# A planned kernel for RWKV-6 attention and a MetaFormer block: new durations of transfers, a new count of TensorE's instructions and a new table of shifts in its planner

## Chip, cores and metric

The kernel runs on one core of one Trainium2 chip. The metric is device time in microseconds of one execution; lower is better. The core has five engines that work side by side: TensorE (PE, with its weight loads shown as PEld), VectorE (DVE), ScalarE (ACT), GpSimd (POOL) and SyncE (SP), which here only issues transfers (DMA). Each engine takes its instructions strictly in the order in which they were written; between engines they wait for each other by semaphores.

## The reference

What is computed, cut to what matters:

```python
# r, k, v, w: (B=4, H=8, S=768, D=48), u: (8, 48)
state = np.zeros((B, H, D, D))
for t in range(S):
    cur = np.einsum('bhd,bhe->bhde', u[None] * kt, vt)
    y[:, :, t] = np.einsum('bhd,bhde->bhe', rt, state + cur)
    state = wt[:, :, :, None] * state + np.einsum('bhd,bhe->bhde', kt, vt)
x = y.transpose(0, 2, 1, 3).reshape(4, 768, 384)
mu, var = x.mean(-1), x.var(-1)            # per token
xn = (x - mu) / np.sqrt(var + 1e-6) * g_ln
out = x + np.maximum(xn @ w_ch1, 0) @ w_ch2   # w_ch1: (384, 1536), w_ch2: (1536, 384)
```

## The kernel before, in words

**Rounds.** The tokens are worked through in eight rounds of 384 tokens (four batches, two halves each). A round has two units of four heads. Round 0 is split into a first tile of 128 tokens and the other 256, so that its names carry the first token tile, as in `h_ps_0_1` (hidden group 0, tiles 1 and 2).

**Attention of a round (`front`).** w, k and r are loaded as they lie (`nat`), turned by TensorE (`w_ps`, `k_ps`, `r_ps`) and copied back by ScalarE. Within a chunk of 64 tokens the products of decays are built in six levels. At each level TensorE makes small products of r and k (`quads`, in the profile `a<-r,k` with 63, 62, 60, 56, 48 or 32 rows, 48 products for a whole round), VectorE multiplies k and r by the decays of that level (`grow`: `k<-k,tot`, `r<-r,tot`), and VectorE keeps the level's squares under a mask (`keep`: `A<-mask,a`). A level's quads need the `grow` of the level before. k is then turned once more (`kn_ps`), `states` makes products of k and v (`a<-v,k`) and a scan on VectorE (`s<-s,decay,a`), and `outputs` adds all up (`a<-v,A`, `a<-sx,rx`, `a<-s,r`). The term with u (`own`: `rk`, `own`, `vo`) needs no TensorE. All these small products use four parts of TensorE's array at a time; the planner calls them `tiled`. They share two homes in PSUM (tag `a`).

**The MLP of a round (`norm`, `mlp`).** VectorE normalises x to `xn`; TensorE turns it (`xT_ps`), ScalarE scales it (`xf`). In round 0 the first product is in float32 (`h_ps<-xf,w`), in later rounds it is made of three products in a rounded format (`hd_ps<-xd,d`, `h_ps<-xhl,wl`, `h_ps<-xhl,wh`), for which the difference weights `d` are streamed from DRAM. The second product is float32 up to round 4 (`o<-ffn,h`) and of three parts in the last three rounds (`a<-w2d,hD` and the like, `o_2D`, `o_2P`). The weights themselves come as pairs of words (`raw`) and are put together by three ScalarE and two VectorE operations each (`convert`: `w<-w,held`, later `ffn<-ffn,rest`).

**The planner.** Nothing is issued in the order of the Python loops. Each operation is given to `plan.add` with an engine (or a choice of VectorE and GpSimd, `EITHER`), a duration, what it reads and writes, an urgency `pri`, and for transfers a latency `lat` and a `size`, the time by which it holds up the transfers behind it. `add` also adds the shift from the table `SHIFTS` whose key is the urgency rounded down. `order` then plays the engines through: of the operations that can start within `WAIT[engine]` of the earliest, it takes the most urgent, and issues it. So each duration, latency, size and shift decides only the order in which each engine's instructions are written.

Four things in `order` matter here. A change of mode on TensorE, between tiled and full products, makes an operation less urgent by `STAY`. Tiled operations are planned `MARGIN` behind their operands. `fetches` models TensorE's instruction supply: every `PIECE` = 256 instructions a new piece has to be there, and a piece takes `FETCH`. And where TensorE would stand still for more than 0.4 us in the first 90 us of the plan, `idle` fills the time with products of zeros (`idle<-nought`), counted in units of 128 columns.

Of the kernel before, what the change touches and what calls it, by code (L numbers as in the profile page):

```python
# [35 lines left out]
class InOrder:  # L36


    waits, last = [], None
# [27 lines left out]
class Plan:  # L67
# [11 lines left out]

    HOP, MARGIN, FILLED, PATIENCE, STAY = 0.1, 0.293159, 60.0, 2.0, 2.0
    BEFORE, PIECE, FETCH, CROWD = 66, 256, 4.11468, 300
    WAITS = 1.006
    DRAIN = {True: 0.1, False: 0.12}
    WAIT = {"PE": 0.0617605, "ACT": 0.155358, "DVE": 0.170848, "POOL": 0.403865, "SP": 0.0}

    SHIFTS = {  # L90
        -232: 14, -216: -4.5, -38: -42, -37: 5, -33: 10.5, -31: -22, -28: -9, -20: 13, -14: -23,
        3: -45, 5: -19.5, 10: -35, 12: 4.5, 14: 4, 21: 8, 22: 29.5, 38: 17.5, 51: 68.5, 52: 30,
        53: -5.5, 54: 24, 55: 4, 58: -30, 62: -4, 63: 26, 66: 2.5, 90: -16, 92: 7.5, 101: -19,
        104: 56, 121: -39, 127: 29.5, 129: 59.5, 136: -23, 142: 8.5, 160: -5, 169: 47, 176:
        -27.5, 182: 14, 207: 7.5, 208: 31, 215: -17.5, 246: 0.5, 247: -12.5, 248: 2.5, 249: -35,
        257: -3.5, 262: 31, 284: 12, 289: 8.5, 306: 4.5, 319: -23.5, 403: 15, 405: 32.5, 409:
        121.5, 412: -52, 417: 8, 418: -16, 425: -2.5, 445: 2.5, 447: 72, 449: -25, 450: -9.5,
        451: 14.5, 454: 3.5, 457: 66.5, 459: 88.5, 462: -10, 463: 5, 479: -74, 483: 8.5, 492: 2,
        493: 22, 497: 64.5, 498: 25.5, 501: 22.5, 502: -8.5,
    }  # L100

    def __init__(self, homes, dynamic):
# [37 lines left out]
    def order(self, busy, idle=None, until=0.0):  # L140
# [16 lines left out]
        dma, todo, out, tiled = 0.0, len(ops), [], False  # L157
        count, ahead = self.BEFORE, 0.0
# [19 lines left out]

        def fetches(t, op):

            waits, after = 0.0, ahead
            for at in range(-int(count) % self.PIECE, op.count, self.PIECE):
                now = t + waits + op.costs["PE"] * at / op.count
                waits += max(after - now, 0.0)
                after = max(now, after) + self.FETCH
            return waits, after

        def switching(t, op):
# [4 lines left out]
        while todo:  # L193
            best = None
            for e, waiting in ready.items():
                at = [(t, op) for op in waiting if (t := start_of(op, e)) is not None]
                if not at:
                    continue
                first = min(t for t, _ in at)
                t, op = min(  # L200
                    ((t, op) for t, op in at if t <= first + self.WAIT[e]),
                    key=lambda x: (x[1].pri + (switching(*x) if e == "PE" else 0), x[1].i),
                )
# [3 lines left out]
            t, op, e = best  # L207
            if idle and e == "PE" and t < until and t - free["PE"] > 0.4 and self.homes[idle[0]]:
                n = int((t - free["PE"]) / (idle[1] * (2 if t < 5.0 else 1)))
# [10 lines left out]
            if e == "PE":  # L220
                fetched, ahead = fetches(t, op)
# [55 lines left out]
def kernel(  # L277
# [12 lines left out]
    nc = tc.nc  # L290
# [11 lines left out]
    U = H // NH  # L302
# [29 lines left out]
    plan = Plan(HOMES | {"a": 2, "b": 4}, ("a", "b"))  # L332
# [107 lines left out]
    def urgent(part, stage):  # L440
        rnd, c0, nc = part
        return at(rnd - (nc == 1), stage)
# [31 lines left out]
    def load_first(nm, part, eng, pri):  # L474
        _, c0, nc = part
        b, f = rounds[0]
        name = natural(nm, part, 0)[0]
        queue = SP if eng == "SP" else ACT
        row, margin = row_of(part)

        def go():
            queue.dma_start(
                out=tiles[name][:, margin : margin + H * row].rearrange("p (h x) -> p h x", h=H),
                in_=SRC[nm][b, :, ds(f * RN + c0 * P, nc * P)]
                .rearrange("h (p c) d -> p h (c d)", p=P),
            )

        plan.add(eng, 0.5, go, w=[name], r=[], pri=pri, lat=2.0, size=0.8 + 0.3 * (nc > 1))

    def load(nm, q):  # L490
        b, f, g = units[q]
        name = f"nat_{nm}{q}"

        def go():
            to = tile_("nat", name, None)
            if q // U < ROWS:
                SP.dma_start(
                    out=to[:, 0 : NH * ROW].rearrange("p (h x) -> p h x", h=NH),
                    in_=SRC[nm][b, ts(g, NH), ds(f * RN, RN)]
                    .rearrange("h (p c) d -> p h (c d)", p=P),  # L500
                )
                return
            for c in range(TT):
                SP.dma_start(
                    out=by_tile(to)[:, c, :, 0:D],
                    in_=SRC[nm][b, ts(g, NH), ds(f * RN + c * P, P)].rearrange("h p d -> p h d"),
                )

        cost_, size = (0.5, 0.8) if q // U < ROWS else (1.65, 1.2)
        plan.add(  # L510
            "SP", cost_, go, w=[name], new=[("nat", name)], pri=at(q // U, "wrk".index(nm)), lat=2.0,
            size=size,
        )
# [309 lines left out]
    def load_v(q, part):  # L823
        _, c0, nc = part
        b, f, g = units[q]
        name, swapped = f"v{q}", f"vx{q}"

        def go():
            t = tile_("v", name, [P, NH, TT, D])
            for c in range(c0, c0 + nc):  # L830
                SP.dma_start(
                    out=t[:, :, c],
                    in_=v[b, ts(g, NH), ds(f * RN + c * P, P)].rearrange("h p d -> p h d"),
                )

        def swap():
            t, src = tile_("vx", swapped, [P, NP, TT, D]), tiles[name]
            cols = slice(c0 * D, (c0 + nc) * D)
            for i in range(2):
                SP.dma_start(  # L840
                    out=t[ds(C * (1 - i), C)].rearrange("p r c d -> p r (c d)")[..., cols],
                    in_=src[ds(C * i, C)]
                    .rearrange("p (r j) c d -> p r j (c d)", j=2)[:, :, 1, cols],
                )

        share = nc / TT
        plan.add(
            "SP", 0.1 + 1.6 * share, go, w=[(name, c0)], new=[] if c0 else [("v", name)],
            pri=urgent(part, 16), lat=2.0, size=share,
        )  # L850
        plan.add(
            "SP", 1.25, swap, r=[(name, c0)], w=[(swapped, c0)], new=[] if c0 else [("vx", swapped)],
            pri=urgent(part, 17), lat=2.3, size=0.3 + 0.7 * share,
        )

    def own_term(q, part):
# [300 lines left out]
    def convert(i):  # L1157
        value_, src, key = parts[i]
        raw_ = f"raw{i}"
# [38 lines left out]

        pri = CONVERT + i / 100
        first = -6 if i < FC // 2 else pri  # L1200
        plan.add("SP", 0.4, fetch, w=[raw_], new=[("raw", raw_)], pri=pri - 24, lat=2.0, size=1.05)
        plan.add(
            "ACT", 0.52, upper, r=[raw_], w=[key], new=[("w2", key)] if i >= FC else [], pri=pri,
        )
# [8 lines left out]
    def halve(g):  # L1213
# [44 lines left out]
        for kc in range(KC):  # L1258
            plan.add(
                "ACT", 0.5, lambda kc=kc: up(kc), r=[rest_[kc]], w=[(l_, kc)],  # L1260
                new=[("w1", l_)] if kc == 0 else [], pri=pri,
            )
            plan.add(
                EITHER, (0.56, 1.1), lambda e, kc=kc: diff(e, kc), r=[(h_, kc), (l_, kc)],
                w=[diff_[kc]], new=[("rest", diff_[kc])], pri=pri,
            )
            plan.add(
                "SP", 0.5, lambda kc=kc: store(kc), r=[diff_[kc]], w=[("w1d", g, kc)], pri=pri,
                lat=2.5, size=1.0,
            )  # L1270

    def halve2(f):
# [59 lines left out]
    def thirds(rnd, f):  # L1332
# [34 lines left out]
        for i in range(TT):  # L1367
# [49 lines left out]
            if last:  # L1417
                plan.add("DVE", 0.53, add, r=[keys[1]] + whole, w=[(x_, "sum", i)], pri=EVICT)
                plan.add("DVE", 0.53, rest, r=[keys[0], (x_, "sum", i)], w=[(x_, "out", i)], pri=EVICT)
                plan.add("SP", 0.36, store, r=[(x_, "out", i)], pri=EVICT, lat=2.0, size=1.0)  # L1420

    def first_product(part):
        rnd, c0, nc = part
# [24 lines left out]
    def mlp(rnd):  # L1448
# [3 lines left out]
        for f in range(FC):  # L1452
# [39 lines left out]
            def relu(h_=h_):  # L1492
# [6 lines left out]
            )  # L1499
            plan.add("ACT", 0.45, copy, r=[ps_d], w=[h_], pri=EVICT)  # L1500
            plan.add(
                "PE", 1.12, go, count=12,
                r=[(f"wl{g}", kc) for kc in range(KC)] + [(f"wh{g}", kc) for kc in range(KC)]
                + [key for kc in range(KC) for key in x_keys(rnd, kc)[:2]]
                + [ps_d if rnd < LAST else ps_d + "t"],
# [9 lines left out]
        for i in range(TT):  # L1515
# [32 lines left out]

            whole = x_of(rnd, i)
            plan.add("DVE", 0.53, add, r=[o] + whole, w=[(x_, "out", i)], pri=EVICT)  # L1550
            plan.add("SP", 0.36, store, r=[(x_, "out", i)], pri=EVICT, lat=2.0, size=1.0)

    def front(part):
# [9 lines left out]
        if rnd == c0 == 0:  # L1565
            plan.add(
                "SP", 0.6, lambda: SP.dma_start(
                    out=u_bc,
                    in_=bass.AP(tensor=u.tensor, offset=u.offset, ap=[[0, P], [D, H], [1, D]]),
                ), w=["u_bc"], pri=5, lat=2.0, size=3.3,  # L1570
            )
            plan.add(
                EITHER, (1.3, 1.6), lambda e: BY[e].memset(a_bufs[1], 0.0), w=[("A1", 0, 0)], pri=32
            )
            for lev in range(NLEV - 1):
                plan.add(
                    "POOL", 1.7, lambda lev=lev: build_mask(lev), r=["wide"], w=[("mask", lev)],
                    pri=lev - 40, port=False,
                )
# [114 lines left out]
```

## Time and profile before

| | us |
|---|---|
| median of three timed runs | 530.34 (530.22 to 533.26) |
| profiled execution | 528.18 |
| its span, on which all times of the profile are counted | 526.2 |
| TensorE busy | 514.0 (8984 products) |
| VectorE busy | 398.5 |
| ScalarE busy | 268.4 |
| GpSimd busy | 82.4 |
| mean granted clock of TensorE | 0.996 |

A row of the profile gives the operation as output<-inputs with the buffers' numbers left out, the shape, and durations. All instructions come from one helper line (L50), so rows are told apart by names. A product in float32 is executed as two passes and is counted as two; a transpose or a product in the rounded format is one. Durations of products on TensorE overlap, so that what one costs is read from start to start: 0.109 us for a transpose of 128 columns, 0.22 for a first product of 128 columns (both passes), 0.43 for one of 256, 0.174 for one of 384 columns in the rounded format. "issue" as the cause of idle time means that the engine waited for nothing that the profile shows.

### The profile page before, as it was taken

How to read it: one execution, taken by the hardware profiler on the slowest of the kernel's cores; microseconds unless marked ns; L12 is line 12 of the kernel's file. 1: busy time of each engine (PE TensorE's matmuls, PEld its weight loads, DVE VectorE, ACT ScalarE, POOL GpSimd, SP SyncE). 2: the span in 40 equal slices, each digit the busy share in tenths (PEclk: the TensorE clock that was granted, in tenths of full speed). 3: DMA queues.
4: the chain of work that ended last, by engine and by line, in shares of the span. 5: the costliest groups of instructions: out<-in, count | busy, mean ns of one | idle time of the engine just before them, and what ended most of it. 6: DMA issues, size and time to landing. Idle time of an engine off the chain costs nothing.

```text
span 526.2 us, 20613 instructions
## 1 busy us (share of the span) xinstructions
PE 514.0 (98%) x8984; PEld 434.7 (83%) x8984; DVE 398.5 (76%) x839; ACT 268.4 (51%) x602; POOL 82.4 (16%) x112
## 2 busy tenths in 40 slices
PE   8999799999999999999999999999999999999996
PEld 6788588677899777899767899758966999999996
DVE  5988959989998998989896597715754876655645
ACT  3788768865385342574440873505930533432321
POOL 6304020071332320131200130000300000000000
PEclk9999989999999999999999999999999999999999
DMA  9855977158836614666401324104201422322201
GB/s 218 249 168 126 224 184 194 31 124 203 244 73 123 161 39 97 134 137 132 133 19 35 94 76 112 34 15 128 57 17 45 123 61 66 99 75 75 77 1 45
DMA packets 122361, 55.83 MB, mean 106 GB/s; under 512 B 93984, under 2 KB 119200, under 8 KB 122272
## 3 DMA queue, kind: packets, MB, share of 16 engines
q1 hardware_dynamic: 119152, 53.54, 40.3%
q10 hardware_dynamic: 3120, 0.98, 0.9%
q8 instruction: 70, 1.15, 0.9%
q14 instruction: 19, 0.16, 0.1%
HBM read 45.05 MB, written 7.10 MB: 99 GB/s over the span
## 4 chain that ended last, share of the span: by engine, by line
PE 93%; DVE 3%; POOL 1%; issue 1%; DMA 1%; ACT 0%; DVEq 0%; POOLq 0%
PE a L50 25%; PE o L50 22%; PE h_ps L50 21%; PE hd_ps L50 9%; PE r_ps L50 3%; PE k_ps L50 3%; PE w_ps L50 3%; PE o_2P L50 2%; PE kn_ps L50 2%; PE xT_ps L50 1%; PE idle L50 1%; PE o_2D L50 1%; DMA nat<-in_k_dram 1%; DVE k L50 1%; POOL rk L50 1%
## 5 line engine op out<-in xcount | busy, mean ns | idle before, releaser
L50 PE MATMUL o<-ffn,h 128*128 128x384 f32 x360 | 123.8, 490 | 0.0
L50 PEld LDWEIGHTS o<-ffn,h 128*128 128x128 f32 x360 | 65.7, 190 | 38.2
L50 ACT COPY h<-hd_ps 128x384 f32<-128x384 f32 x84 | 40.2, 479 | 83.3 <-PE hd_ps L50 79.9
L50 PEld LDWEIGHTS a<-r,k 48*63 48x63 f32 (+5 forms) x4608 | 63.4, 126 | 15.6 <-issue 7.5
L50 PE MATMUL a<-r,k 48*63 48x32 f32 (+5 forms) x4608 | 69.5, 212 | 2.7 <-issue 1.7
L50 DVE SCALAR_TENSOR_TENSOR h<-h_ps,h 128x384 f32<-128x384 f32 x84 | 46.4, 555 | 32.8 <-PE h_ps L50 30.7
L50 PE MATMUL h_ps<-xhl,wl 128*128 128x384 f32 x252 | 59.7, 345 | 0.0
L50 PE MATMUL h_ps<-xhl,wh 128*128 128x384 f32 x252 | 57.7, 336 | 0.0
L50 PE MATMUL hd_ps<-xd,d 128*128 128x384 f32 x252 | 56.5, 349 | 0.0
L50 DVE TENSOR_TENSOR k<-k,tot 112x768 f32<-112x768 f32 (+1 forms) x50 | 40.3, 807 | 8.4 <-PE a L50 5.9
L50 PEld LDWEIGHTS h_ps<-xhl,wh 128*128 128x128 f32 x252 | 45.2, 188 | 0.0
L50 PEld LDWEIGHTS hd_ps<-xd,d 128*128 128x128 f32 x252 | 43.7, 188 | 1.8 <-ACT w L50 0.2
L50 PEld LDWEIGHTS h_ps<-xhl,wl 128*128 128x128 f32 x252 | 44.1, 188 | 1.2 <-ACT r L50 0.2
L50 ACT ACTIVATE h<-h 128x384 f32<-128x384 f32 x48 | 25.1, 525 | 36.6 <-DVE h L50 36.4
L50 DVE COPY_PREDICATED A<-mask,a 128x768 f32<-128x768 int8 (+2 forms) x36 | 39.5, 1096 | 2.5 <-PE a L50 2.3
L50 DVE TENSOR_TENSOR r<-r,tot 112x768 f32<-112x768 f32 (+1 forms) x50 | 39.6, 793 | 0.0
L50 ACT ACTIVATE hH<-h 128x384 fp32r<-128x384 f32 x36 | 18.5, 525 | 32.2 <-DVE h L50 24.4
L50 DVE SCALAR_TENSOR_TENSOR hL<-h,hH 128x384 fp32r<-128x384 f32 x36 | 20.0, 554 | 12.0 <-ACT hH L50 11.5
L50 POOL TENSOR_TENSOR rk<-nat,nat 128x576 f32<-128x576 f32 (+1 forms) x13 | 17.8, 1372 | 65.9 <-DVE ffn L50 20.9
L50 DVE TENSOR_TENSOR x<-o,x 128x384 f32<-128x384 f32 x15 | 8.3, 554 | 25.1 <-PE o L50 25.1
L50 PE MATMUL h_ps<-xf,w 128*128 128x128 f32 (+1 forms) x144 | 27.1, 342 | 0.0
L50 ACT COPY A<-a 32x384 f32<-32x384 f32 (+2 forms) x36 | 15.5, 432 | 19.4 <-PE a L50 19.1
(121 smaller groups left out, 1022.9 us busy)
## 6 DMA issues: line engine op xcount, KB each, us to landing
d<-w1d SPq DMA_DIRECT2D x84, 192.0 KB, 3.0
raw<-in_moe_w_ch_dram SPq DMA_DIRECT2D x24, 384.0 KB, 3.8
v<-in_v_dram SPq DMA_DIRECT2D x48, 96.0 KB, 3.1
out_dram<-x SPq DMA_DIRECT2D x24, 192.0 KB, 2.1
nat<-in_w_dram SPq DMA_DIRECT2D x36, 96.0 KB, 3.5
nat<-in_k_dram SPq DMA_DIRECT2D x36, 96.0 KB, 3.2
nat<-in_r_dram SPq DMA_DIRECT2D x36, 96.0 KB, 3.0
w1d<-w1diff SPq DMA_DIRECT2D x12, 192.0 KB, 2.6
```

The source lines that it names most:

```text
L50: ins = self.tc.keep_in_program_order(f(*args, **kw))
```

## The change

The change edits numbers of the planner, and in `fetches` the way in which the start of the next piece of instructions is counted. `STAY` goes from 2.0 to 6.8, `MARGIN` from 0.293 to 0.197, `PATIENCE` from 2.0 to 4.3; `WAIT` changes for each engine. Most transfers get another `size` (loads of w, k and r 1.6 instead of 1.2 in later rounds, raw weights 1.3 instead of 1.05, v 1.6 instead of 1.0 for a whole round, stores 0.65 instead of 1.0), the first loads another latency (3.5 instead of 2.0). The table `SHIFTS` is replaced as a whole, 77 entries by 92. No operation is added or taken away by hand.

```diff
-    HOP, MARGIN, FILLED, PATIENCE, STAY = 0.1, 0.293159, 60.0, 2.0, 2.0
-    BEFORE, PIECE, FETCH, CROWD = 66, 256, 4.11468, 300
+    HOP, MARGIN, FILLED, PATIENCE, STAY = 0.1, 0.196918, 60.0, 4.33011, 6.79752
+    BEFORE, PIECE, FETCH, CROWD = 66, 256, 3.98109, 300
-    WAIT = {"PE": 0.0617605, "ACT": 0.155358, "DVE": 0.170848, "POOL": 0.403865, "SP": 0.0}
+    WAIT = {"PE": 0.0354766, "ACT": 0.217982, "DVE": 0.140393, "POOL": 0.485775, "SP": 0.0207245}
     SHIFTS = {
-        -232: 14, -216: -4.5, -38: -42, -37: 5, -33: 10.5, -31: -22, -28: -9, -20: 13, -14: -23,
+        -537: -0.5, -535: -6.5, -520: -4, -457: -8, -337: 9.5, -296: 10.5, -295: 5.5, -200: -2,
...
-            waits, after = 0.0, ahead
-            for at in range(-int(count) % self.PIECE, op.count, self.PIECE):
-                now = t + waits + op.costs["PE"] * at / op.count
+            waits, after, n = 0.0, ahead, op.count * self.WAITS
+            at = (self.PIECE - count % self.PIECE) % self.PIECE
+            while at < n:
+                now = t + waits + op.costs["PE"] * at / n
                 waits += max(after - now, 0.0)
                 after = max(now, after) + self.FETCH
+                at += self.PIECE
...
-        plan.add(eng, 0.5, go, w=[name], r=[], pri=pri, lat=2.0, size=0.8 + 0.3 * (nc > 1))
+        plan.add(eng, 0.5, go, w=[name], r=[], pri=pri, lat=2.0 if c0 else 3.5, size=1.05 + 0.5 * (nc > 1))
...
-        cost_, size = (0.5, 0.8) if q // U < ROWS else (1.65, 1.2)
+        cost_, size = (0.5, 1.05) if q // U < ROWS else (1.65, 1.6)
...
-            pri=urgent(part, 16), lat=2.0, size=share,
+            pri=urgent(part, 16), lat=2.0, size=1.6 * share,
-            "SP", 1.25, swap, r=[(name, c0)], w=[(swapped, c0)], new=[] if c0 else [("vx", swapped)],
-            pri=urgent(part, 17), lat=2.3, size=0.3 + 0.7 * share,
+            "SP", 1.3, swap, r=[(name, c0)], w=[(swapped, c0)], new=[] if c0 else [("vx", swapped)],
+            pri=urgent(part, 17), lat=2.2, size=0.2 + 0.5 * share,
...
-        plan.add("SP", 0.4, fetch, w=[raw_], new=[("raw", raw_)], pri=pri - 24, lat=2.0, size=1.05)
+        plan.add("SP", 0.4, fetch, w=[raw_], new=[("raw", raw_)], pri=pri - 24, lat=2.0, size=1.3)
...
-                lat=2.5, size=1.0,
+                lat=2.3, size=0.7,
...
-                plan.add("SP", 0.36, store, r=[(x_, "out", i)], pri=EVICT, lat=2.0, size=1.0)
+                plan.add("SP", 0.36, store, r=[(x_, "out", i)], pri=EVICT, lat=2.0, size=0.65)
...
-                "PE", 1.12, go, count=12,
+                "PE", 1.11 if rnd < LAST else 1.05, go, count=12,
...
-                ), w=["u_bc"], pri=5, lat=2.0, size=3.3,
+                ), w=["u_bc"], pri=5, lat=2.0, size=1.5,
```

## The prediction

> **What bounds the kernel now.** I read the page first, for the share of each engine. TensorE is busy 98% of the span, and its clock is granted in full in every slice but the sixth.
>
> ```profile
> PE 514.0 (98%) x8984; PEld 434.7 (83%) x8984; DVE 398.5 (76%) x839; ACT 268.4 (51%) x602; POOL 82.4 (16%) x112
> ...
> PEclk9999989999999999999999999999999999999999
> ```
>
> So the sum of products bounds it, and only three things can move: TensorE's idle time, its clock, and what its order itself costs. The view of TensorE's waits has the named idle time; its longest entries all lie before 68 us:
>
> ```profile
> PE a L50 <- issue: 1.7, 2, 1.2
> PE k_ps L50 <- DMA nat<-in_k_dram: 1.6, 2, 1.3
> PE a L50 <- DVE r L50: 0.8, 1, 0.8
> ```
>
> TensorE's timeline gives them a place (start, duration, instruction; in brackets the idle time before it):
>
> ```profile
> 60.35 1.39 PE L50 MATMUL a<-r,k 48*60 48x32 f32 x82 [0.78 <-DVE r L50]
> 62.97 0.41 PE L50 MATMUL a<-r,k 48*60 48x32 f32 x14 [1.23 <-issue]
> 63.31 1.56 PE L50 MATMUL h_ps<-xf,w 128*128 128x256 f32 x6
> 66.16 0.61 PE L50 MATMUL k_ps<-ident,nat 128*112 128x128 f32 x2 [1.29 <-DMA nat<-in_k_dram]
> ```
>
> One block waits for VectorE, then in its middle for its own instructions ("issue"), and then TensorE, which takes its work in order, stands before the transposes of k until their load lands. The view by stretches of 3.41 us (length, busy time of PE, PEld, DVE, ACT, POOL, granted clock, DMA share, GB/s) shows what follows:
>
> ```profile
> 61.14:64.55 3.41, 2.18 (x61) 1.85 (x53) 3.17 (x9) 2.02 (x4) 0.00 (x0) 1.00 0.83 172
> 64.55:67.96 3.41, 1.76 (x12) 1.09 (x11) 1.82 (x5) 0.85 (x3) 0.00 (x0) 1.00 0.97 223
> 67.96:71.37 3.41, 3.28 (x17) 2.91 (x16) 1.77 (x3) 1.63 (x6) 0.00 (x0) 0.50 0.86 227
> ```
>
> After the poorly filled stretch the clock is 0.50 for 3.41 us. From start to start, TensorE loses here 0.9 us (VectorE), 1.3 (issue), 2.2 (the load of k: pauses of 1.67, 0.68 and 0.29 us where 0.22, 0.11 and 0.11 are usual) and 1.7 (half of 3.41, the clock): **6.1 us between 59 and 72 us**. From 80 us on, the waits view has only two entries, of 0.3 and 0.2 us. Ahead of 59 us VectorE is the bound: from 10.33 us, when the first w is copied, to 58.65 us, the end of the last normalised tile of round 0, its own waits come to 3.7 us in all.
>
> **What the change does.** No edited number is executed; each moves the planner's order. Of the operations, only TensorE's filler products (idle<-nought) grow, from 12 to 18, and six operations go from GpSimd to VectorE on balance. All 351 transfers and all real products stay, so I sum over the order.
>
> *Start.* The first loads get a planned landing 1.5 us later, so six filler products of 384 columns stand ahead of the first transposes, where two stood. The timeline of the start:
>
> ```profile
> 0.99 2.50 PE L50 MATMUL idle<-nought 128*128 128x384 f32 x4 [0.99 <-DVE eps L50]
> 4.34 1.93 PE L50 MATMUL r_ps<-ident,nat_r 128*112 128x128 f32 x8 [0.85 <-POOL wide L50]
> ...
> 10.33 1.96 PE L50 MATMUL w_ps<-ident,nat 128*112 128x128 f32 x16
> ```
>
> Eight transposes take 1.93 us at 4.34 and sixteen take 1.96 at 10.33: the clock is half until about 10 us. Each filler product is two passes, so there are 12, at about 0.65 us cold (from 2.50 us for four shorter ones) and 0.33 warm. If the clock stayed half until 9.9 us as in this row, they would end at 8.9 us, and the 24 transposes, which ended at 9.5, near 11.9: +2.4 us. The Trainium skill (TensorE: Matmul & The Clock Gate, part "The HAM clock gate") holds instead that about 3.4 us of sustained work release the clock, at a phase that a free-running window sets. The fillers have no pause, where the row has one of 0.85 us; so full speed would come between 4.4 and 7.8 us. With 6.1, about 7.7 passes are cold and 4.3 warm: the end is at 7.5 us, the transposes' at 7.5 + 24 x 0.11 = 10.1. I take the rule, as the row is not uninterrupted work: **+0.6 us** (-0.4 to +2.4).
>
> *VectorE to the end of round 0's normalising.* Added up with the durations of the same forms in the trace, its rows up to that tile are 56.2 us before and 57.1 after, +1.0. Against it, the scans (s) waited 1.4 us for TensorE and 0.4 for ScalarE; conversions of w_2 and w_3 now stand between. I put the two at **0** (-1 to +1.5).
>
> *TensorE's work done by then.* While VectorE holds the pace, TensorE's own work is free. Ahead of the transposes of x it now has three more first products (9 products x 0.22 = 2.0), six transposes fewer (-0.65) and a change of mode more (+0.33, below): **-1.7 us** for all that follows.
>
> *The stall at 60 to 67 us.* In the new order two groups of transposes of w and the first wide product (0.65 + 1.3 us) precede the block that waited 0.9 us for VectorE. Behind that block come three narrow first products (2.0) and a wide one (1.3) before the transposes of k, and their load stands at the same place behind as many others in SP's queue. It landed near 67.1 us; TensorE reaches it near 67.6. So the 2.2 us go. What takes their place: the next block (56x32) is planned only 11 us behind, and VectorE's rows up to its operands, with the conversions of ffn_0 to ffn_3 among them, come to 11.3. I leave 0.9 us there and 1.3 for the issue, of whose price no row with another spacing tells me more (0 to 2). The stretch before k is then filled to 80% or more.
> Does the clock stay? The skill's rule (same page, "HAM oscillation") is that idle gaps over about 3.4 us must be avoided. By the rule nothing is gained here, as the longest gap was 1.29 us and the clock should never have fallen. By the rows, a stretch 52% filled (1.76 of 3.41) was enough, and one 64% filled (2.18) was not. I take the rows: the 1.7 us go. Together 6.1 - 2.4 = **-3.7 us** (by the rule -2.0).
>
> *Changes of mode.* STAY is raised, yet TensorE passes 164 times between small concurrent products (a<-r,k, a<-v,k, a<-v,A) and full ones, where it passed 148 times. The chain of waits shows the price:
>
> ```profile
> 138.56 1.25 PE hd_ps L50 x6
> ...
> 161.96 1.45 PE a L50 x96
> ...
> 173.27 1.51 PE a L50 x96
> ...
> 242.50 2.83 PE a L50 x192
> ...
> 357.11 1.05 PE hd_ps L50 x6
> ```
>
> Six products that follow a small block take 1.25 us, others 1.05: 0.20. Two blocks of these kinds alone take 1.45 + 1.51, joined 2.83: 0.13. That is 0.33 per pair. Eight pairs more, one counted above: 7 x 0.33 = **+2.3 us**. It is on the path, since TensorE is full there.
>
> *Margins.* MARGIN falls from 0.293 to 0.197: each small block is planned 0.1 us nearer to its operands. Up to about 250 us VectorE's summed rows run about 2 us or more ahead of TensorE's in both orders, except at the blocks named, so I put **+0.5 us** (0 to 2). Six operations more on VectorE (0.6 to 1 us each) lie in that lead; without it they would cost up to 5 us.
>
> *End.* Behind the last first product six groups of second products cover VectorE's and ScalarE's last conversions where seven did (0.52 each): 3.1 us against a chain of about 3.3. The last store is reached by the same two VectorE rows: 0 (to +0.5).
>
> **Sum:** +0.6 + 0 - 1.7 - 3.7 + 2.3 + 0.5 + 0 = **-2.0 us**. Against the profiled execution (528.18 us, span 526.2) that is 526.2; the median of the timed runs is 530.34, 2.2 above it, so I forecast **528.3**. About 1% (5.3 us) is what a measurement of this kernel can tell from no change.
>
> **Rivals.**
> *A, the whole head closes.* The clock is released early (-1.0 against my +0.6), the issue stall (1.3), the wait at the 56x32 block (0.9) and the margin (0.5) are nothing as well: -5.7, **524.6**. For it: the issue stalls stand in long runs of small products, which are now more often interrupted. Against it: the seven pairs stay.
> *B, slower: the conversions come in front of TensorE.* VectorE waited 2.9 and 2.5 us for ScalarE's parts of ffn here, behind a full TensorE. In the new order ffn_0 to ffn_3 stand ahead of the operands of the 56x32 block, and ScalarE does part of it only after copies that wait for TensorE. If these 5.4 us come onto the path for the 0.9 (+4.5), the stretch is empty again and the clock falls (+1.7), and the start costs 1.2: -2.0 + 6.8 = +4.8, and with the longer fillers +5.4, **535.7**. It decides from a wait of 2.9 us at that block on: there the gain is used up. Against it: ScalarE is busy for only 2.7 of the 8 us from 64 to 72.
> *C, the load of k stays late.* Earlier small loads push it behind again; 2.2 and 1.7 stay: +1.9, **532.2**. For it: the DMA share is 0.83 to 0.97 there. Against it: the same number of transfers stands ahead.
> That the change does nothing is excluded: the orders part from TensorE's eleventh group on.
>
> **How the numbers follow.** Forecast 0.52, A 0.20, B 0.14, C 0.14. Most of A lies below 525.0: with a little of the forecast's tail, faster 0.20. B straddles 535.6, and unseen stalls add to it: slower 0.14. The rest is 0.66. The range takes in most of A and C and the start's bad end, and leaves half of B out: 523.8 to 534.5; the forecast's own is 526 to 531.
>
> **What would show it.** Right: no entry for a load of k among TensorE's waits, granted clock 1.00 from 60 to 80 us, first block of small products near 10.3 us, TensorE some 4 to 5 us further by 80 us, and about 2.3 us of it given back later in groups of 1.25 us. Wrong: a clock of 0.50 after 20 us, a wait of over 2 us for VectorE near 70 us, or idle time of TensorE behind 100 us.

## The result, and the profile after

| | before | after |
|---|---|---|
| median of eight timed runs, us | 530.28 (527.78 to 533.26) | 527.97 (526.07 to 530.06) |
| profiled execution, us | 528.18 | 526.92 |
| its span, us | 526.2 | 525.2 |
| mean granted clock in it | 0.996 | 1.000 |
| TensorE busy, us (products) | 514.0 (8984) | 515.8 (8996) |
| VectorE busy, us | 398.5 | 403.6 |
| GpSimd busy, us | 82.4 | 72.2 |

The ratio of the times is **0.9942, with a 95% interval from 0.9916 to 0.9968**: some 3 us less, between 1.7 and 4.5. The forecast was 528.3 us, 2.0 less. The two profiled executions are only 1.26 us apart; each is one draw from its own spread (5.5 us before, 4.0 after). They can therefore show where time went and where it came from, and not how large the whole gain is.

The page after, in the lines that answer to the two shown of before: busy time, share of the span and number of instructions of each engine, and the granted clock in 40 slices.

```profile
PE 515.8 (98%) x8996; PEld 434.5 (83%) x8996; DVE 403.6 (77%) x845; ACT 269.8 (51%) x602; POOL 72.2 (14%) x106
...
PEclk9999999999999999999999999999999999999999
```

TensorE's share is the same. The gap in the sixth slice of its clock has gone. The twelve more products are the six more fillers, of two passes each. The whole view of TensorE's waits after (engine, what waited, what it waited for, us in all, times, longest):

```profile
PE idle L50 <- DVE eps L50: 1.0, 1, 1.0
PE r_ps L50 <- DMA nat<-in_r_dram: 0.7, 1, 0.7
PE w_ps L50 <- ACT held L50: 0.7, 1, 0.7
PE a L50 <- DVE hD L50: 0.7, 1, 0.7
PE a L50 <- issue: 0.6, 2, 0.3
PE xT_ps L50 <- DVE xn L50: 0.4, 1, 0.4
PE a L50 <- DVE x L50: 0.3, 1, 0.3
PE a L50 <- ACT sx L50: 0.2, 1, 0.2
```

The 1.6 us for a load of k and the 0.8 for VectorE's r are not there any more, and "issue" has fallen from 1.7 to 0.6 us. New are 0.7 us for a load of r, 0.7 for a copy of ScalarE's (held) at 41.94 us and 0.7 for hD. The place of the stall, in TensorE's timeline after (start, duration, instruction, in brackets the idle time before it):

```profile
62.31 0.27 PE L50 MATMUL xT_ps<-ident,xn 128*128 128x128 f32 x1
62.72 0.91 PE L50 MATMUL w_ps<-ident,nat 128*112 128x128 f32 x6
63.46 1.54 PE L50 MATMUL h_ps<-xf,w 128*128 128x256 f32 x6
64.94 1.52 PE L50 MATMUL a<-r,k 48*60 48x32 f32 x96
66.39 3.57 PE L50 MATMUL h_ps<-xf,w 128*128 128x128 f32 x24
69.80 0.99 PE L50 MATMUL k_ps<-ident,nat 128*112 128x128 f32 x6
70.63 1.46 PE L50 MATMUL h_ps<-xf,w 128*128 128x256 f32 x6
71.93 0.38 PE L50 MATMUL r_ps<-ident,nat 128*112 128x128 f32 x2
73.04 0.32 PE L50 MATMUL r_ps<-ident,nat 128*112 128x128 f32 x1 [0.73 <-DMA nat<-in_r_dram]
```

The block of 96 small products at 64.94 has no pause within it and none before it. 24 passes of narrow products (12 products, some of them moved here) lie in front of the transposes of k, which start at 69.80 and find their load there. The only pause left is 0.73 us for r. The same 13.6 us in stretches of 3.41 us (length, busy time of PE, PEld, DVE, ACT, POOL, granted clock, DMA share, GB/s):

```profile
61.14:64.55 3.41, 2.91 (x18) 2.26 (x18) 3.38 (x7) 3.40 (x9) 0.00 (x0) 1.00 0.98 239
64.55:67.96 3.41, 3.41 (x113) 3.04 (x112) 3.24 (x8) 2.79 (x7) 0.00 (x0) 1.00 0.98 271
67.96:71.37 3.41, 3.41 (x23) 2.91 (x22) 3.41 (x6) 2.77 (x9) 0.00 (x0) 1.00 0.86 164
71.37:74.78 3.41, 2.68 (x16) 2.05 (x14) 2.07 (x5) 2.29 (x6) 0.00 (x0) 1.00 0.92 239
```

Where before TensorE was busy for 1.76 of 3.41 us and then ran at half clock, it is now busy for the whole of that stretch, and the clock stays at 1.00.

**Where the time goes, over the whole span.** Idle time alone does not add up here, as TensorE's queue takes up what other engines lose. So both orders were put on one scale: the work that TensorE has finished, counted as the sum of the usual start-to-start times of its products, with fillers counted as nothing. Other weights move single rows by a few tenths of a us up to about one; the swing of the lead between 45 and 75 us, and what is left of it at the last product, stay. The table has the time at which each execution reaches the same amount of work.

| work done, us | before at | after at | after is ahead by |
|---|---|---|---|
| 5 | 12.38 | 12.98 | -0.60 |
| 25 | 41.01 | 45.11 | -4.10 |
| 35 | 55.23 | 56.11 | -0.88 |
| 40 | 64.18 | 63.64 | +0.54 |
| 45 | 73.28 | 68.98 | +4.31 |
| 50 | 78.29 | 75.20 | +3.08 |
| 80 | 109.93 | 106.93 | +3.00 |
| 150 | 184.90 | 180.86 | +4.04 |
| 350 | 395.83 | 393.30 | +2.53 |
| last product | 521.88 | 520.35 | +1.52 |

The lead comes into being between 60 and 75 us. Of the 3.08 us that are there at 75 us, 1.56 are given back over the remaining 445, and the end of the span takes another 0.5. Amounts between the points vary with the order (after is 4.1 us behind at 45 us, where it has put other work first), so only steps between places at which both orders have much the same work behind them are read as gains or losses.

### The profile page after: what moved, and what is told of

Its sections match the earlier page's. It is cut to its first block, busy times and chain, and to the rows that moved or that the text cites. A ratio compares the mean times of both kernels' runs of the same rounds, so it can differ in the third digit from the quotient of the medians.

```text
span 525.2 us, 20616 instructions
## 1 busy us (share of the span) xinstructions
PE 515.8 (98%) x8996; PEld 434.5 (83%) x8996; DVE 403.6 (77%) x845; ACT 269.8 (51%) x602; POOL 72.2 (14%) x106
## 4 chain that ended last, share of the span: by engine, by line
PE 88%; DMA 4%; DVE 3%; POOL 2%; ACT 1%; issue 0%; SPq 0%; POOLq 0%; DVEq 0%
PE a L50 24%; PE o L50 23%; PE h_ps L50 21%; PE hd_ps L50 9%; PE o_2P L50 2%; PE w_ps L50 2%; PE r_ps L50 2%; DMA nat<-in_w_dram 2%; PE kn_ps L50 2%; PE k_ps L50 2%; PE xT_ps L50 1%; PE o_2D L50 1%; DVE x L50 1%; DMA own<-own_d 1%; DVE w L50 1%; POOL wide L50 1%
## 5 line engine op out<-in xcount | busy, mean ns | idle before, releaser
L50 PEld LDWEIGHTS a<-r,k 48*60 48x60 f32 (+5 forms) x4608 | 63.3, 126 | 15.4 <-issue 7.4
L50 PE MATMUL a<-r,k 48*60 48x32 f32 (+5 forms) x4608 | 69.6, 212 | 0.9 <-issue 0.6
L50 PE MATMUL h_ps<-xhl,wl 128*128 128x384 f32 x252 | 61.1, 350 | 0.0
L50 DVE TENSOR_TENSOR k<-k,tot 112x768 f32<-112x768 f32 (+1 forms) x50 | 41.7, 833 | 16.7 <-PE a L50 13.9
L50 PE MATMUL a<-w2d,hD 128*128 128x384 f32 x72 | 24.6, 342 | 0.7 <-DVE hD L50 0.7
L50 PEld LDWEIGHTS a<-v,A 64*64 64x64 f32 x384 | 20.5, 133 | 5.4 <-issue 2.0
```

The costliest lines, as they stand in the source:

```text
L50: ins = self.tc.keep_in_program_order(f(*args, **kw))
```

## The experiments: what the two traces tell apart, and what was not tried

No further kernel was run for this case, so no cause below was isolated by undoing a part of the change on the chip. What follows are comparisons within the two traces and within the eight timed runs; they can support or contradict a step, which is less than an experiment does.

**VectorE's instructions beside GpSimd's, and alone.** The prediction put nothing for VectorE's own durations changing. Each VectorE instruction that stands as a row of its own in the two timelines, and whose form does so at least three times while GpSimd stands still, was compared with the median of these times. Of 867 instructions with no GpSimd work beside them, 5 are more than 0.2 us longer than that median, all of them predicated copies. With at least 0.3 us of GpSimd work beside them, it depends on what VectorE reads:

| instruction beside at least 0.3 us of GpSimd work | cases | over 0.2 us longer |
|---|---|---|
| two operands, none straight from a product (k<-k,tot, w<-w,held, vo<-v,own, w1diff<-wh,wl and the like) | 20 | 14 |
| the predicated copy A<-mask,a | 17 | 9 |
| all others (h<-h_ps,h, A<-a,mask_and, x<-o,x, stats<-x and the like) | 64 | 0 |

Rows in which the timeline joins several instructions are left out of the table, and one kind of them does not fit its last line: three xn<-x,mv,rstd in a row, which read one tensor each, usually take 1.25 us, but 3.30 at 172.29 us before, where GpSimd's vo and rk run beside them.

VectorE's timeline after has four long ones, at 14.73, 22.80, 43.94 and 51.88, and a usual one at 22.45 (the form of 14.73 is too rare to be among the cases of the table; before, it took 0.55 and 0.54 us alone):

```profile
14.73 1.20 DVE L50 TENSOR_TENSOR rk<-rk,u_bc 128x384 f32<-128x384 f32 x1
...
22.45 0.42 DVE L50 TENSOR_TENSOR k<-k,tot 112x256 f32<-112x256 f32 x1
22.80 1.23 DVE L50 TENSOR_TENSOR r<-r,tot 112x256 f32<-112x256 f32 x1
...
43.94 1.17 DVE L50 TENSOR_TENSOR k<-k,tot 112x256 f32<-112x256 f32 x1
...
51.88 1.20 DVE L50 CUSTOM_DVE_ANT_0 w<-w,held 128x768 uint16<-128x768 uint16 x1
```

And GpSimd's timeline for the same places:

```profile
14.48 1.04 POOL L50 TENSOR_TENSOR tot<-w 112x512 f32<-112x512 f32 x1 [2.19 <-DVE r L50]
...
22.52 1.22 POOL L50 TENSOR_TENSOR rk<-nat,nat 128x384 f32<-128x384 f32 x1 [0.30 <-DVE tot L50]
...
43.41 1.42 POOL L50 TENSOR_TENSOR rk<-nat,nat 128x576 f32<-128x576 f32 x1 [4.75 <-DMA nat<-in_r_dram]
51.60 1.07 POOL L50 TENSOR_TENSOR vo<-v,own 128x384 f32<-128x384 f32 x1 [6.78 <-DMA nat<-in_w_dram]
```

At their starts GpSimd's instructions have 0.79, 0.94, 0.89 and 0.79 us left (the second: 22.52 + 1.22 - 22.80). The long ones exceed their usual 0.55, 0.42, 0.42 and 0.56 us by 0.65, 0.81, 0.75 and 0.64: in each of the four by 0.13 to 0.15 us less than what GpSimd has left, as if the work waited for its end. The Trainium skill (GPSIMD Engine Reference, "Specifications") names such a conflict: the two engines share their interfaces to the memory on the chip, and VectorE's instructions with two inputs there, or in a mode that takes two ports, contend for them. The first and third row agree with it; whether xn runs in such a mode no view shows. The six of 20 that stay short (one began 0.07 us before GpSimd's instruction, at 22.45) and the two kinds of outcome of the predicated copy, of which 5 of 44 are long with GpSimd standing still, are not explained by it. That the work beside them makes them long is a correlation of two traces: no kernel was run in which only GpSimd's part was moved.

**The same rows of VectorE, summed alike in both orders.** The working of the prediction put 56.2 us before against 57.1 after, but these are unlike sums: the first has the durations as they ran, the second the usual ones. With the usual duration of each form in both, it is 54.64 us before and 57.14 after. The traced excess over the usual durations is 1.5 us before and 3.5 after. So the order itself gave VectorE 2.5 us more to do before the last normalised tile of round 0, and the longer instructions are about 2 us more; about 0.6 of the excess is a predicated copy in both orders, and nearly all the rest stands beside GpSimd's work. Such sums count twice where instructions overlap. By the trace VectorE was busy for 43.2 of the 48.2 us from its first instruction behind the first small products to the end of that tile before (10.33 to 58.56), and for 47.4 of 50.7 us after (11.12 to 61.77): 4.2 us more work, 1.8 less idle time.

**The clock: could it still fall in the new order?** Five of the eight timed runs after have a mean clock of 0.999 or 1.000 and average 527.1 us; three have 0.996 to 0.998 and average 529.1. A stretch of 3.41 us at half clock lowers the mean by 1.7 / 526 = 0.003, so it looks as if the clock fell once in those three. The traces show another source of such a mean: the clock also falls after the last product, where it costs nothing. Four stretches, the first and third of before, the second and fourth of after (columns as above):

```profile
59.56:62.97 3.41, 1.41 (x84) 1.28 (x83) 3.31 (x8) 3.35 (x8) 0.00 (x0) 1.00 0.93 251
58.11:61.52 3.41, 2.54 (x102) 1.95 (x100) 3.34 (x12) 2.76 (x7) 2.55 (x4) 1.00 0.63 116
525.35:526.18 0.83, 0.00 (x0) 0.00 (x0) 0.00 (x0) 0.00 (x0) 0.00 (x0) 0.50 0.00 0
518.37:521.79 3.42, 2.15 (x13) 1.83 (x11) 2.63 (x6) 0.00 (x0) 0.00 (x0) 1.00 0.15 58
```

The mean of before, 0.996, holds 1.7 us of the stall and 0.4 of the last 0.83 us. In the profiled run after, the clock falls at 525.20, as the span ends; in a run whose stretches begin at another time, up to about 3.4 us of the end could be at half clock (an estimate from the fourth row: with 2.15 us of products the clock stayed), which takes 0.003 off the mean. That covers two of the three runs and nearly the third. The first two rows are the least filled stretches of this length that can be laid anywhere between 10 and 515 us: 1.41 us of products before, 2.54 after, while 2.18 and 2.15 were enough to keep the clock. So if the filling decides, the new order keeps its clock wherever the stretches begin, provided that it runs as in the trace, and the old one depends on where they begin: the stretch with 1.41 lay across two of those that count (61.14 is the border), and the clock fell only after the one with 1.76. Which of the two sources the three runs have is not known, as only the profiled runs have a trace; why they are 2.0 us longer is open.

**What was not tried,** and would tell the terms apart. The stall alone: in the kernel before, one load planned later, which on TensorE moves only two groups of transposes of k and one of r behind first products.

```diff
-pri=at(q // U, "wrk".index(nm)), lat=2.0,
+pri=at(q // U, "wrk".index(nm)), lat=5.0 if (nm, q) == ("k", 5) else 2.0,
```

The clock alone: the same order with filler products ahead of those transposes, so that the stretch before them is full though the load is as late. The start: the new order with 8 units of filler in place of 18. That last one is also what these traces suggest as a better version, since the first 0.72 us are lost to fillers; whether 8 units release the clock as early is open. Taking the new sizes of transfers, the new count of instructions or the new shifts alone was not tried either; each gives an order that parts from both others near the start.

## Why the prediction was right, and where it was not

The sum came out close (-2.0 forecast, -1.0 between the spans of the profiled pair, about -3 by the ratio). It did so with one term wrong by more than 2 us, and two others that made up for it. That the place and the kind of the gain were right is the forecast's own; that the sum comes so close is luck.

| step | forecast, us | measured in the profiled pair, us |
|---|---|---|
| start | +0.6 | +0.72 |
| VectorE to the end of round 0's normalising | 0 | +2.3 |
| TensorE's work done by then | -1.7 | -1.35, and a change of mode (0.33) in it: -1.7 of products |
| the stall at 60 to 67 us | -3.7 | -4.75 |
| changes of mode and margins | +2.8 | +1.56 |
| end | 0 (to +0.5) | +0.5 |
| sum | -2.0 | -1.0 |

**Start: right, with its reason.** The first small products begin at 10.33 us, where 9.61 was their time before. TensorE's timeline of the start:

```profile
0.99 6.79 PE L50 MATMUL idle<-nought 128*128 128x384 f32 x12 [0.99 <-DVE eps L50]
7.62 1.03 PE L50 MATMUL r_ps<-ident,nat_r 128*112 128x128 f32 x8
8.49 1.04 PE L50 MATMUL k_ps<-ident,nat 128*112 128x128 f32 x8
9.37 1.04 PE L50 MATMUL w_ps<-ident,nat 128*112 128x128 f32 x8
10.33 0.66 PE L50 MATMUL a<-r,k 48*63 48x32 f32 x32
```

Eight transposes take 1.03 us at 7.62, where before they took 1.93 at 4.34: they are at full clock. The trace's record of the granted clock begins with the full clock at 6.37 us, within the fillers, where before it began at 9.93; the view by stretches shows 1.00 ahead of it too, so that the half speed there can be read only from the durations. The forecast had chosen the rule of the Trainium skill (TensorE: Matmul & The Clock Gate, "The HAM clock gate"), about 3.4 us of sustained work on a free-running window (4.4 to 7.8 us), over the older row, in which the clock was half until about 10 us with a pause of 0.85 us in the work. Here the rule was the better guide. The two moments are one period of 3.41 us and 0.15 us apart, so the profiled pair has nearly the same borders of its stretches; other runs need not.

**VectorE: the step that failed.** Counted from the first small products, the last transposes of x of round 0 come 2.3 us later than before (they start at 62.31 where they started at 59.30; 0.72 of the 3.0 us is the start). The forecast had +1.0 us of work and -1.0 of waits. The waits did fall, and further than forecast; the scan's 1.4 us for TensorE is gone. The view of VectorE's waits from 10 to 80 us after:

```profile
DVE A L50 <- POOL wide L50: 4.3, 1, 4.3
DVE ffn L50 <- ACT ffn L50: 1.0, 1, 1.0
DVE A L50 <- PE a L50: 0.6, 2, 0.3
DVE tot L50 <- POOL tot L50: 0.4, 2, 0.3
DVE k L50 <- PE a L50: 0.4, 1, 0.4
DVE ffn L50 <- ACT rest L50: 0.3, 1, 0.3
DVE r L50 <- PE r_ps L50: 0.3, 1, 0.3
```

The first entry is that of the start and ends at 11.12 us, about when the first copy of w is there anyway. The two for ffn lie behind 70 us. The others together are 1.7 us, where before they were 3.7. So the loss is not in waits but in work: VectorE was busy for 4.2 us more and idle for 1.8 less, 2.4 in all. By the sums above the work is 2.5 us of more instructions and about 2 of longer ones. The error was to compare a sum of durations as they ran with a sum of usual durations. It halved the added work, and it hid that the durations as they ran go with what GpSimd does at the same time.

**TensorE's work done by then: right.** It is 39.11 us at those transposes where it was 37.76.

**The stall: right in place and mechanism, and larger.** From the transposes of x to 50 us of work, TensorE took 18.99 us for 12.24 of work before, and 12.89 us for 10.89 after: 6.75 us lost, then 2.0. Gone are the wait for k and the half clock, as forecast. Of the 2.4 us that the forecast left, the 0.9 at the block with 56 rows did not come, and "issue" fell further than assumed; a wait of 1.0 us from start to start for r came in. Of the loss before, the clock is 1.6 us (3.28 us of products ran at half speed from 67.96 on), the late load 2.2, near the forecast's 1.7 and 2.2. Rival B, the conversions of ffn in front of TensorE, can be read off the waits above: VectorE's waits for ScalarE there were to come onto the path, but of 2.9 and 2.5 us only 1.0 and 0.3 are left. Rival C, the load of k late again, has no entry. Of rival A, the head that closes altogether, the block with 56 rows and part of "issue" came true, but not its earlier start, and VectorE's added work took more than these gave. Between the rule of the Trainium skill on idle gaps (TensorE: Matmul & The Clock Gate, "HAM oscillation": none over about 3.4 us) and the row of the half-filled stretch, the row was taken, and the profiled execution kept its clock once the stretch was full. That is consistent with the row; it does not prove that the filling decides, since no run changed it alone.

**Modes and margins: right in kind, smaller.** The chain of waits after shows the same price:

```profile
133.16 1.21 PE a L50 x96
134.37 1.26 PE hd_ps L50 x6
...
137.72 1.06 PE hd_ps L50 x6
```

The six products behind a small block take 1.26 us, others 1.06. But behind 80 us there are 59 blocks of small products against 54, five pairs more and not seven: 5 x 0.33 = 1.65 us, beside 1.56 measured. The 1.56 is what is left over behind 75 us, whatever its cause, so the agreement supports the price and does not show it alone. The forecast had taken all changes of mode over the whole order but one to lie behind the head. The lower margin shows no more than a small price (0.5 forecast): behind 80 us TensorE's waits are 0.7 us in all against 0.5. After, it is one new wait, in TensorE's timeline:

```profile
417.09 0.34 PE L50 MATMUL o_2P<-w2h,hH 128*128 128x384 f32 x1
418.08 0.45 PE L50 MATMUL a<-w2d,hD 128*128 128x384 f32 x1 [0.65 <-DVE hD L50]
```

**End.** From the last product to the end of the span it is 4.85 us where it was 4.3, at the upper end of the forecast.

**The signs.** No wait for a load of k, a clock of 1.00 from 60 to 80 us and a first block at 10.33 us came as named. The lead of 4 to 5 us by 80 us was 3.1 (4.3 for a moment at 69 us), and 1.6 of it, not 2.3, was given back. Of the signs of being wrong only a trace came: 0.65 us of idle time at 418 us.

**What stays open.** The difference between the profiled pair (1.3 us) and the ratio (about 3, at least 1.7) is not explained by any step; the spread of single runs is large enough to hold it. How often each order loses its clock in the head was not measured.

## What to carry to other kernels

Where one engine is full, put both orders on a scale of work done and look for the place where the lead comes into being; here one late load and the half clock that followed it (3.8 us) held more than the whole gain, and 98% busy on the page hid it. When two orders are compared by adding durations, take the same kind of duration on both sides, and see whether a neighbour that works at the same time makes them longer. A mean clock of a run counts the end as well, where a fall costs nothing: look where it falls. A plan that weighs each operation alone does not see what GpSimd's work may cost on VectorE.

## What the runs showed of the hardware

- VectorE instructions with two operands such as k and tot took 0.2 to 0.9 us longer in 14 of 20 cases beside GpSimd's work, in the longest ones by nearly what GpSimd had left (0.42 us became 1.17 and 1.23). The predicated copy did so in 9 of 17 cases beside it and in 5 of 44 without it; none of 64 other instructions in rows of their own did, but three xn in a row did once (3.30 us for 1.25).
- A stretch of 3.41 us in which TensorE was busy for 1.76 us was followed by 3.41 us at half clock, though its longest pause was 1.29 us; stretches busy for 2.18 us (before) and for 2.15, 2.68 and 2.91 (after) were not.
- Uninterrupted products from 0.99 us on brought the full clock at 6.37 us; with a pause of 0.85 us among them it came at 9.93. There the stretch that ended at 6.53 us was busy for 2.56 of 3.41 us and did not bring it, though less (2.18) was enough to keep it later.
- "issue" pauses within blocks of small products were 1.7 us before and 0.6 after, with 59 against 54 such blocks behind 80 us; that the one makes the other was not tried.
